# A gated linear attention with two mixture layers: fewer weight conversions in the attention front, a three-step schedule for the second chunk, and another order in the gate

## The chip, the cores and the metric

The kernel runs on one core of one Trainium2 chip. The metric is the time of one execution on the device in microseconds (us). Three runs of the kernel before gave 1474.3, 1478.15 and 1478.42, median 1478.15. A separate execution was profiled; it took 1473.71 us.

## The reference

Attention with a gated state, per batch and head, 768 steps, head size 48:

```
f = 1 / (1 + exp(-f_logit))
state = f[t] * state + outer(k[t], v[t]);   y[t] = q[t] @ state
```

The heads are laid side by side (384 columns, 3072 tokens). Then a first layer with a rational activation, and a second with four experts:

```
h = x @ w_in                                  # 384 -> 2048
g = (a0 + a1 h + a2 h^2 + a3 h^3) / (1 + |b0||h| + |b1| h^2 + 1e-6)
x = g @ w_out                                 # 2048 -> 384
p = probs / (sum(probs) + 1e-9)
out = sum over e of p[:, e] * (relu(x @ w1[e]) @ w2[e])   # 384 -> 1024 -> 384
```

All is float32. The weights of the first layer (w_in, w_out) arrive as pairs of 32-bit words and have to be turned into float32 on the chip.

## The kernel before, in words

The tokens are cut into six chunks of 128 time steps by four batches (512 columns each). Per chunk the kernel does attention in four blocks (one per batch), the first layer in 16 slots of 128 hidden columns, and the second layer in 4 x 8 slots. A matmul in full precision is made of three passes: an operand is split into a high part (ScalarE) and the rest (GpSimd for weights, VectorE for activations), and high x high, low x high, high x low are summed; so a slot's first or second product of 128x512 is nine matmuls. Weights that are used again are stored to DRAM in split form ("ws<-w") and read back.

One loop runs over steps v from -25 to 192, with tau = v + 19. It emits the instructions of all engines by hand, in this order; each engine runs its own in order, so a wait on one engine holds what is behind it. There are three parts.

- *Front*, tau -6 to -2: Att.first takes the four blocks of the first chunk, one per step, with the block before finishing in the same step. On VectorE: w, scans, the first halves of the step's conversions, the masking of the old block, newton1, newton2, q_hat, the second halves of the conversions, finish. k_hat (k times g) and the conversion's last product are on GpSimd. warm() issues matmuls with no use for their result. The block after the next is loaded at the end of a step by SP, behind the step's stores.
- *Fill*, tau -1 to 18: the first layer on the first chunk with plain float32 matmuls, one slot per step: fill_in(tau + 1), then fill_out(tau - 2), six matmul instructions each; the rational gate (gate_in on ScalarE, gate_step on VectorE and ScalarE) lies between: a tile is "new" in one step and "old" in the next. Slot j needs its converted weights at tau = j - 1. CONV1 gives the step of each slot's conversion. A conversion has a first half (L731, L732 on VectorE, L733, L734 on ScalarE) and a second half (L736, L737 on VectorE, the product at L739, a store to w1s, and for odd slots the load of the next raw pair).
- *Main*, v from -1: step v emits in2 (v + 1) and out2 (v - 1) of the second layer, and where first_mix_steps says, in1 and out1 of the first layer for the next chunk, whose gate runs in gate_step. The attention of chunks 1 to 5 is threaded in: Att.t0 gives a block's start step and Att.stage what it issues k steps later: k = 1 exp, w, scans; 2 inverse, k_hat (GpSimd), newton1, newton2; 3 q_hat (GpSimd); 4 scores and masking; 5 and later the transposes of k, the y products, the update of the state and the transposes of y. PA is threaded between the matmuls of the step's first in2, PB between those of out2; DVE1, ACT0, ACT1, POOL1 and REST are places in the step for the other engines. loads() issues f at k = -1, k and q at k = 0, v at k = 2.

Chunk 1 starts a block every two steps from v = -4 and uses two PSUM banks, 6 and 7: scores in both, then the transposes of k in 6 and y in 7, then the update in 6 and the transposes of y in 7. Bank 5 belongs to in1 (h1), and in the fill banks 5 to 7 hold the gate's q. Weights for the main part are loaded from tau = 10 on.

Of the kernel before, what the change touches and what calls it, by code (L numbers as in the profile page):

```python
# [8 lines left out]
F32 = mybir.dt.float32  # L9
F32R = mybir.dt.float32r  # L10
# [3 lines left out]
ALU = mybir.AluOpType  # L14
# [3 lines left out]
NB, NH, S, D = 4, 8, 768, 48  # L18
# [4 lines left out]
PR = 112  # L23
# [307 lines left out]

R = 14
AHEAD = 8
CONV1 = (-6, -5, -5, -4, -4, -3, -3, -2, -2, -1, 0, 1, 2, 3, 4, 5)
NRAW = 8
LAST = NCH * NE * NJ2
FILL = NJ1 + 3
# [1 line left out]
PA, PB, ACT0, ACT1, POOL1, DVE1, REST = range(7)  # L339


def first_mix_steps():


    when, groups = {}, {}
    for c in range(1, NCH):
        p = NE * NJ2 * (c - 1)
        if c == 1:
            at = [8, 9, 10, 12, 14, 15, 16, 17, 18, 19, 20, 21, 23, 24, 25, 26]
            ends = (16, 20, 24, 29)  # L350
        else:
            at = [2, 3, 4, 5] if c == 2 else [-1, 1, 3, 5]
            at += [7, 9, 11, 13, 15, 17, 19, 21, 23, 24, 25, 26]
            ends = (8, 16, 24, 29)
        for j, s in enumerate(at):
            when[p + s] = (c, j)
        for n, s in enumerate(ends):
            groups[p + s] = (c, n)
    return when, groups
# [37 lines left out]
class Block:  # L397


    def __init__(self, att, c, b):  # L400
        self.att, self.nc, self.c, self.b = att, att.tc.nc, c, b
        if c == 0:
            self.pa, self.pk, self.py = att.bank_sets[b % 2]
            self.px = self.pk
        else:
            self.pa, self.py = self.pk, self.px = att.pair
        self.last = c == NCH - 1
# [30 lines left out]

    def k_hat(self):
        k = self.k[0:PR]  # L440
        self.nc.gpsimd.tensor_tensor(out=k, in0=k, in1=self.g[0:PR], op=ALU.mult)

    def newton1(self):
        nc, gm, g = self.nc, self.att.gm[0:PR], self.g[0:PR]
# [92 lines left out]
class Att:  # L537
# [16 lines left out]
    @staticmethod  # L554
    def t0(c, b):
        if c == 1:
            return -4 + 2 * b
        if c == 2:
            return 5 + 7 * b
        return NE * NJ2 * (c - 1) - 9 - 8 * (3 - b)  # L560

    def start(self, fetch):
# [80 lines left out]
    def stage(self, blk, k):  # L643
        rs = range(NP)
        if k == 1:
            return {ACT0: [blk.exp], DVE1: [blk.w], REST: [blk.scans]}
        if k == 2:
            return {ACT0: [blk.inverse], POOL1: [blk.k_hat], DVE1: [blk.newton1], REST: [blk.newton2]}
        if k == 3:
            return {POOL1: [blk.q_hat]}  # L650
        if k == 4:
            return {PA: [blk.all_scores], REST: [blk.masked]}
        keys = [] if blk.last else [partial(blk.k_t, r) for r in rs]
        upd = [] if blk.last else [partial(blk.update, r) for r in rs]
        copy = [] if blk.last else [blk.k_copy]
        end = ([] if blk.last else [blk.finish]) + [blk.x_lo]
        xt = [partial(blk.x_t, m) for m in range(3)]
        if blk.c == 1:
            if k == 5:
                return {PA: keys + blk.y_parts(*rs), ACT1: copy + [blk.y_copy], PB: upd + xt, REST: [blk.x_hi] + end}  # L660
            return {}
        if k == 5:
            return {PB: keys + blk.y_parts(*rs), REST: copy}
        if k == 6:
            return {PA: upd, ACT1: [blk.y_copy]}
        if k == 7:
            return {PA: xt, ACT1: [blk.x_hi], REST: end}
        return {}
# [13 lines left out]
def fused(ctx, tc, aps, consts, gm, dp, prep, flag_op):  # L682


    nc = tc.nc
    w1, w2, out = aps["w1"], aps["w2"], aps["out"]
    sc, pn, ident, mask = consts
# [5 lines left out]
    def pool(name, bufs):  # L693
        return ctx.enter_context(tc.tile_pool(name=name, bufs=bufs))

    wp, x2p, sp, op, pbp, tp, osp = (pool(n, k) for n, k in (
        ("wp", R), ("x2p", 2), ("s1p", 1), ("op", 1), ("pbp", 1), ("tp", 2), ("osp", 2)))
    g1p, g2p, gp = pool("g1p", QC1), pool("g2p", 3), pool("gp", 2)
    att = Att(ctx, tc, aps, consts, gm, banks)
# [7 lines left out]
    raw, temp, w1f = {}, {}, {}  # L707
# [3 lines left out]
    def fetch():  # L711
        i = fetched[0]
        if i < NJ1:
            fetched[0] += 2
            pl, tag = (att.xp, "x") if i == 4 else (x2p, "x2")
            t = pl.tile([128, 2, 2 * SW], I32, tag=tag, name="raw")
            for a in range(2):
                raw[i + a] = t[:, a]
                nc.sync.dma_start(out=raw[i + a], in_=w1[i + a].bitcast(I32))

    def conv(i, stage):
        if stage == 0:
            t = spare_pools[i % 3].tile([128, 2 * SW], F32, tag=("o", "s1", "pb")[i % 3], name="t")
            temp[i] = t
        f = temp[i]
        p, m = f[:, 0:SW], f[:, SW:2 * SW]
        pi, mi = p.bitcast(I32), m.bitcast(I32)
        words = raw[i].rearrange("p (n w) -> p n w", w=2)
        lo, hi = words[:, :, 0], words[:, :, 1]
        if stage == 0:  # L730
            nc.vector.tensor_scalar(pi, hi, 0x7FF00000, None, ALU.bitwise_and)  # L731
            nc.vector.tensor_scalar(mi, hi, 0x000FFFFF, None, ALU.bitwise_and)  # L732
            nc.scalar.activation(out=pi, in_=pi, func=AF.Relu, scale=8.0, bias=sc[:, 7:8])  # L733
            nc.scalar.activation(out=m, in_=mi, func=AF.Identity, scale=2.0 ** -20, bias=sc[:, 8:9])  # L734
        else:
            nc.vector.scalar_tensor_tensor(out=pi, in0=hi, scalar=-2 ** 31, in1=pi, op0=ALU.bitwise_and, op1=ALU.bitwise_or)  # L736
            nc.vector.scalar_tensor_tensor(out=m, in0=lo.bitcast(U32), scalar=2.0 ** -52, in1=m, op0=ALU.mult, op1=ALU.add)  # L737
            w1f[i] = wp.tile([128, SW], F32, tag="w", name="wf")
            nc.gpsimd.tensor_tensor(out=w1f[i], in0=m, in1=p, op=ALU.mult)  # L739
            nc.sync.dma_start(out=w1s[i], in_=w1f[i])  # L740
            if i % 2:
                fetch()

    def conv_ops(tau):
        fs = [[], []]
        for i in range(NJ1):
            for k in range(2):
                if tau == CONV1[i] + k * (CONV1[i] > NB - 8):
                    fs[k].append(partial(conv, i, k))
        return fs  # L750

# [51 lines left out]
    x2, hps, act1, act2 = {}, {}, {}, {}  # L803
# [88 lines left out]
    def gate_step(new, old, ops):  # L892

        if old:
            q0, r0, y0, _ = gate.pop(old[:2])
            nc.vector.scalar_tensor_tensor(out=q0, in0=q0, scalar=QC, in1=r0, op0=ALU.add, op1=ALU.mult)  # L896
        if new:
            q, r, y, h = gate[new[:2]]
            nc.vector.scalar_tensor_tensor(out=q, in0=q, scalar=sc[:, 5:6], in1=r, op0=ALU.mult, op1=ALU.add)  # L899
            nc.scalar.activation(out=r, in_=q, func=AF.Ln, bias=sc[:, 6:7])  # L900
            nc.scalar.activation(out=r, in_=r, func=AF.Exp, scale=-1.0)
        if old:
            nc.vector.scalar_tensor_tensor(out=q0, in0=q0, scalar=2.0, in1=r0, op0=ALU.subtract, op1=ALU.mult)
        if new:
            nc.vector.tensor_tensor(out=y, in0=y, in1=h, op=ALU.mult)  # L905
        if old:
            if old[0] == 0:
                gh = g1p.tile([128, 512], F32, tag="gh", name="g")
                nc.vector.scalar_tensor_tensor(out=gh, in0=y0, scalar=sc[:, 3:4], in1=q0, op0=ALU.subtract, op1=ALU.mult)
                act1[old[:2]] = gh  # L910
            else:
                nc.vector.scalar_tensor_tensor(out=q0, in0=y0, scalar=sc[:, 3:4], in1=q0, op0=ALU.subtract, op1=ALU.mult)  # L912
        for f in ops[DVE1]:
            f()
        if new:
            nc.vector.scalar_tensor_tensor(out=y, in0=y, scalar=sc[:, 2:3], in1=h, op0=ALU.subtract, op1=ALU.mult)  # L916
        for f in ops[ACT1] + ops[POOL1]:
            f()
        if old and old[0]:
            gh = g1p.tile([128, 512], F32R, tag="gh", name="gh")  # L920
            gl = g1p.tile([128, 512], F32R, tag="gl", name="gl")
            nc.scalar.copy(out=gh, in_=q0)  # L922
            nc.vector.tensor_tensor(out=gl, in0=q0, in1=gh.bitcast(F32), op=ALU.subtract)  # L923
            act1[old[:2]] = (gh, gl)

# [90 lines left out]
    for v in range(-FILL - 6, LAST + 1):  # L1016
        tau = v + FILL
        ops = att.begin(v)
        if tau == -5:
            prep()  # L1020
        if tau + 6 <= NB:
            att.first(tau + 6, conv_ops(tau) if tau + 6 < NB else [[], []])
# [16 lines left out]
        new = ready[0] if ready else None  # L1039
        if new:  # L1040
            gate_queue.remove(new)
        old, pend_old = pend_old, new
# [5 lines left out]
        c, k = v // (NE * NJ2) - 1, v % (NE * NJ2)  # L1048
# [217 lines left out]
```

## Time and profile before

| | us |
|---|---|
| median of three runs (lowest, highest) | 1478.15 (1474.3, 1478.42) |
| profiled execution, and its span | 1473.71, 1471.9 |
| TensorE busy in the span | 1386.3 (94%) |
| VectorE, ScalarE, GpSimd busy | 907.8, 679.0, 306.3 |
| mean granted TensorE clock | 0.967 of full speed |

PE is TensorE's matmul part, PEld its weight loads, DVE VectorE, ACT ScalarE, POOL GpSimd, SP the engine that issues most DMAs; L731 is line 731 of the kernel before. Busy time of PE counts a matmul at whatever clock it was granted, so a stage with a clock below 1.00 holds less work than its busy time says. Times are from the start of the span.

### The profile page before, as it was taken

How to read it: one execution, taken by the hardware profiler on the slowest of the kernel's cores; microseconds unless marked ns; L12 is line 12 of the kernel's file. 1: busy time of each engine (PE TensorE's matmuls, PEld its weight loads, DVE VectorE, ACT ScalarE, POOL GpSimd, SP SyncE). 2: the span in 40 equal slices, each digit the busy share in tenths (PEclk: the TensorE clock that was granted, in tenths of full speed). 3: DMA queues.
4: the chain of work that ended last, by engine and by line, in shares of the span. 5: the costliest groups of instructions: out<-in, count | busy, mean ns of one | idle time of the engine just before them, and what ended most of it. 6: DMA issues, size and time to landing. Idle time of an engine off the chain costs nothing.

```text
span 1471.9 us, 18283 instructions
## 1 busy us (share of the span) xinstructions
PE 1386.3 (94%) x6502; PEld 1112.8 (76%) x6502; DVE 907.8 (62%) x1395; ACT 679.0 (46%) x1160; POOL 306.3 (21%) x265
## 2 busy tenths in 40 slices
PE   5859989999989999999999999999999999999997
PEld 5723477877768888878888878888878888888885
DVE  7799844678784666575666675666675645562222
ACT  3367623767562644552553552553552643451111
POOL 3232324465643002012001012001012001111010
PEclk8779969999999999999999999999999999999998
DMA  7352635767787566666666565665665766667660
GB/s 259 122 189 79 232 118 189 237 221 250 247 296 257 180 190 204 181 185 219 188 201 189 185 206 179 215 206 186 196 206 174 227 193 194 181 204 235 193 183 24
DMA packets 115699, 287.80 MB, mean 196 GB/s; under 512 B 13104, under 2 KB 31888, under 8 KB 114832
## 3 DMA queue, kind: packets, MB, share of 16 engines
q1 hardware_dynamic: 115024, 286.36, 60.4%
q8 instruction: 54, 0.88, 0.3%
q14 instruction: 45, 0.37, 0.1%
q10 hardware_dynamic: 576, 0.18, 0.0%
HBM read 237.69 MB, written 48.81 MB: 195 GB/s over the span
## 4 chain that ended last, share of the span: by engine, by line
PE 74%; DVE 14%; ACT 3%; DMA 3%; issue 3%; POOL 2%; SPq 1%; ACTq 0%; DVEq 0%; POOLq 0%
PE bank L839 34%; PE bank L829 31%; PE bank L484 2%; PE bank L489 1%; DMA ws<-w 1%; DVE t L737 1%; PE bank L867 1%; POOL w L786 1%; DVE g L431 1%; PE bank L874 1%; DVE t L732 1%; PE bank L460 1%; PE bank L500 1%; DVE q L899 1%; DVE y L905 1%
## 5 line engine op out<-in xcount | busy, mean ns | idle before, releaser
L829 PE MATMUL bank<-x,w 128*128 128x512 f32 x2448 | 616.6, 397 | 9.1 <-DVE gl L932 7.2
L829 PEld LDWEIGHTS bank<-x,w 128*128 128x128 f32 x2448 | 457.0, 190 | 104.4 <-DVE gl L932 9.5
L839 PE MATMUL bank<-gh,w 128*128 128x512 f32 x1632 | 529.6, 400 | 5.0 <-DVE t L968 5.0
L839 PEld LDWEIGHTS bank<-gh,w 128*128 128x128 f32 x1632 | 304.6, 189 | 66.8 <-DVE t L968 5.9
L839 PE MATMUL bank<-gl,w 128*128 128x512 f32 x816 | 324.5, 398 | 0.0
L932 DVE SCALAR_TENSOR_TENSOR gl<-bank,gh 128x512 fp32r<-128x512 f32 x192 | 131.6, 686 | 128.0 <-ACT gh L931 128.0
L969 POOL TENSOR_TENSOR o<-o,t 128x512 f32<-128x512 f32 x69 | 87.4, 1295 | 511.8 <-DVE t L968 511.8
L839 PEld LDWEIGHTS bank<-gl,w 128*128 128x128 f32 x816 | 154.1, 189 | 30.7
L899 DVE SCALAR_TENSOR_TENSOR q<-q,sc,r 128x512 f32<-128x512 f32 x80 | 63.7, 797 | 177.6 <-ACT r L888 177.5
L931 ACT ACTIVATE gh<-bank 128x512 fp32r<-128x512 f32 x192 | 113.7, 594 | 125.2 <-PE bank L829 125.2
L786 POOL TENSOR_TENSOR w<-rawbuf,w 128x384 fp32r<-128x384 f32 x96 | 105.3, 1121 | 102.5 <-ACT w L785 76.0
L922 ACT CAST gh<-q 128x512 fp32r<-128x512 f32 x80 | 49.6, 620 | 157.5 <-DVE q L912 156.8
L883 ACT COPY h<-bank 128x512 f32<-128x512 f32 x80 | 46.9, 586 | 133.1 <-PE bank L829 132.5
L484 PEld LDWEIGHTS bank<-v,am 128*128 128x128 f32 x384 | 70.7, 221 | 22.1 <-DVE am L471 17.5
L484 PE MATMUL bank<-v,am 128*128 128x48 f32 x384 | 65.2, 282 | 16.9 <-DVE am L471 16.9
L923 DVE TENSOR_TENSOR gl<-q,gh 128x512 fp32r<-128x512 f32 x80 | 55.4, 692 | 36.3 <-ACT gh L922 35.7
L968 DVE TENSOR_TENSOR t<-bank,pb 128x512 f32<-128x512 f32 x69 | 46.0, 687 | 42.4 <-PE bank L839 23.1
L986 DVE TENSOR_TENSOR s<-s,bank 128x512 f32<-128x512 f32 x45 | 30.6, 682 | 66.9 <-PE bank L839 66.9
L867 PE MATMUL bank<-x,wf 128*128 128x512 f32 x96 | 48.8, 649 | 20.0 <-DVE y L916 19.3
L534 POOL TENSOR_TENSOR s<-am,i 48x192 f32<-48x192 f32 x32 | 16.3, 510 | 240.2 <-DVE am L533 239.0
L896 DVE SCALAR_TENSOR_TENSOR q<-q,r 128x512 f32<-128x512 f32 x80 | 66.0, 825 | 0.0
L900 ACT ACTIVATE r<-q,sc 128x512 f32<-128x512 f32 x80 | 58.0, 725 | 17.1 <-DVE q L899 9.1
(100 smaller groups left out, 1495.6 us busy)
## 6 DMA issues: line engine op xcount, KB each, us to landing
w<-ws SPq DMA_DIRECT2D x448, 384.0 KB, 3.6
ws<-w SPq DMA_DIRECT2D x96, 384.0 KB, 3.8
raw<-in_w_dram SPq DMA_DIRECT2D x16, 768.0 KB, 6.9
rawbuf<-in_w_dram SPq DMA_DIRECT2D x64, 192.0 KB, 3.5
f<-in_qkf_dram SPq DMA_DIRECT2D x24, 256.0 KB, 3.7
k<-in_qkf_dram SPq DMA_DIRECT2D x24, 256.0 KB, 4.0
q<-in_qkf_dram SPq DMA_DIRECT2D x24, 256.0 KB, 4.2
w1s<-wf SPq DMA_DIRECT2D x16, 384.0 KB, 5.6
```

Of the source, the lines that this page charges most:

```text
L484: self.nc.tensor.matmul(self.py[:, o:o + D], self.am[a][:, r], self.v[:, o:o + D], start=(self.c == 0 and r == 0 and a == 0), stop=(r == N ...
L786: nc.gpsimd.tensor_tensor(out=t[:, 1], in0=r, in1=t[:, 0].bitcast(F32), op=ALU.subtract)
L829: nc.tensor.matmul(ps, a[:, o], b[:, kk, :], start=(n == 0), stop=(n == 8))
L839: nc.tensor.matmul(acc[m], a[:, o], b, start=(start and n == 0), stop=(stop and n == last))
L867: nc.tensor.matmul(ps, w[:, kk * 128:(kk + 1) * 128], att.x[0][:, kk, :], start=(kk == 0), stop=(kk == 2))
L896: nc.vector.scalar_tensor_tensor(out=q0, in0=q0, scalar=QC, in1=r0, op0=ALU.add, op1=ALU.mult)
L899: nc.vector.scalar_tensor_tensor(out=q, in0=q, scalar=sc[:, 5:6], in1=r, op0=ALU.mult, op1=ALU.add)
L900: nc.scalar.activation(out=r, in_=q, func=AF.Ln, bias=sc[:, 6:7])
L923: nc.vector.tensor_tensor(out=gl, in0=q0, in1=gh.bitcast(F32), op=ALU.subtract)
L931: nc.scalar.activation(out=gh, in_=h, func=AF.Relu)
L932: nc.vector.scalar_tensor_tensor(out=gl, in0=h, scalar=0.0, in1=gh.bitcast(F32), op0=ALU.max, op1=ALU.subtract)
L969: nc.gpsimd.tensor_tensor(out=o[c][:, m], in0=o[c][:, m], in1=t, op=ALU.add)
```

## The change

1. CONV1: the first four conversions go one to each of the front's steps (before: one, two, two, and two first halves), the other twelve are spread over tau -2 to 13. Those of the front do their last product on VectorE, and so does k_hat for chunk 0.
2. Chunk 1's blocks start every three steps from v = -6 and use banks 5, 6 and 7: scores in 5 and 7, the transposes of k in 6, y in 7, update in 5, transposes of y in 6. The transposes of k and the y products move from PA to PB of k = 5; update and the rest move to k = 6. The scores are threaded after the first matmul of the in2 group, not after the ninth. in1 of chunk 1 runs at steps 10, 11, 12, 13 where it was 8, 9, 10, 12; chunk 2's blocks start at 6, 12, 19, 26 where it was 5, 12, 19, 26.
3. gate_step issues the old tile's operations first, with its copy to gh right behind, then ACT1, then the new tile's, then DVE1 and POOL1, and gl last.

```
-CONV1 = (-6, -5, -5, -4, -4, -3, -3, -2, -2, -1, 0, 1, 2, 3, 4, 5)
+CONV1 = (-6, -5, -4, -3, -2, -1, 0, 1, 3, 4, 5, 7, 8, 9, 11, 12)
...
-            at = [8, 9, 10, 12, 14, 15, 16, 17, 18, 19, 20, 21, 23, 24, 25, 26]
+            at = [10, 11, 12, 13, 14, 15, 16, 17, 18, 19, 20, 21, 23, 24, 25, 26]
...
+        elif c == 1:
+            self.pa, self.pk, self.py = att.bank_sets[0]
+            self.px = self.pk
...
     def k_hat(self):
         k = self.k[0:PR]
-        self.nc.gpsimd.tensor_tensor(out=k, in0=k, in1=self.g[0:PR], op=ALU.mult)
+        eng = self.nc.gpsimd if self.c else self.nc.vector
+        eng.tensor_tensor(out=k, in0=k, in1=self.g[0:PR], op=ALU.mult)
...
         if c == 1:
-            return -4 + 2 * b
+            return -6 + 3 * b
         if c == 2:
-            return 5 + 7 * b
+            return (6, 12, 19, 26)[b]
...
         if k == 4:
-            return {PA: [blk.all_scores], REST: [blk.masked]}
+            return {PA: [blk.all_scores] + [lambda: None] * (8 * (blk.c == 1)), REST: [blk.masked]}
...
         if blk.c == 1:
             if k == 5:
-                return {PA: keys + blk.y_parts(*rs), ACT1: copy + [blk.y_copy], PB: upd + xt, REST: [blk.x_hi] + end}
+                return {PB: keys + blk.y_parts(*rs), REST: copy}
+            if k == 6:
+                return {PA: upd, ACT1: [blk.y_copy], PB: xt, REST: [blk.x_hi] + end}
             return {}
...
-            nc.gpsimd.tensor_tensor(out=w1f[i], in0=m, in1=p, op=ALU.mult)
+            eng = nc.vector if CONV1[i] < NB - 6 else nc.gpsimd
+            eng.tensor_tensor(out=w1f[i], in0=m, in1=p, op=ALU.mult)
...
-                if tau == CONV1[i] + k * (CONV1[i] > NB - 8):
+                if tau == CONV1[i] + k * (CONV1[i] >= NB - 6):
```

gate_step after the change (STT stands for nc.vector.scalar_tensor_tensor):

```
if old:
    STT q0 = (q0 + QC) * r0;  STT q0 = (2 q0 - ...) * r0
    if old[0]: STT q0 = (y0 - a0) * q0;  gh = nc.scalar.copy(q0)
    else:      STT gh = (y0 - a0) * q0;  act1[old[:2]] = gh
ops[ACT1]
if new:
    STT q = q * |b1| + r;  ScalarE Ln, Exp;  y = y * h;  STT y = (y - a1) * h
ops[DVE1], ops[POOL1]
if old and old[0]: gl = q0 - gh
```

## Rows read from the trace of the kernel before

**Rows 1.** Windows by stage: busy us (count) per engine, clock, DMA share, GB/s.
```profile
0.00:68.40 68.40, 44.66 (x288) 42.40 (x288) 49.78 (x91) 26.23 (x40) 18.50 (x17) 0.75 0.56 205
68.40:178.30 109.90, 89.36 (x195) 37.43 (x195) 100.68 (x146) 71.80 (x113) 32.84 (x19) 0.92 0.45 154
178.30:267.20 88.90, 80.45 (x425) 66.88 (x426) 45.16 (x72) 30.80 (x63) 37.50 (x39) 0.85 0.52 176
267.20:430.00 162.80, 151.82 (x735) 124.13 (x733) 122.06 (x171) 111.41 (x206) 91.06 (x83) 0.99 0.72 250
430.00:1400.00 970.00, 958.79 (x4591) 792.10 (x4592) 573.80 (x890) 428.85 (x723) 121.56 (x107) 1.00 0.64 199
```

**Rows 2.** Groups by shape on VectorE, 0 to 67 us: busy us, mean ns, idle before.
```profile
L732 DVE TENSOR_SCALAR t<-raw 128x768 int32<-128x768 int32 x7 | 7.1, 1013 | 0.0
...
L737 DVE SCALAR_TENSOR_TENSOR t<-raw,t 128x768 f32<-128x768 uint32 x5 | 6.4, 1275 | 0.0
...
L736 DVE SCALAR_TENSOR_TENSOR t<-raw,t 128x768 int32<-128x768 int32 x5 | 4.8, 955 | 2.8 <-ACT t L733 2.8
L731 DVE TENSOR_SCALAR t<-raw 128x768 int32<-128x768 int32 x7 | 3.8, 544 | 2.4 <-DMA raw<-in_w_dram 2.4
L424 DVE TENSOR_SCALAR f<-f 112x512 f32<-112x512 f32 x4 | 3.6, 911 | 0.7 <-ACT f L420 0.6
L456 DVE TENSOR_TENSOR q<-q,i 112x512 f32<-112x512 f32 x4 | 2.8, 692 | 0.1
...
L1189 DVE TENSOR_SCALAR psum__65<-psum__65 128x24 f32<-128x24 f32 x1 | 1.7, 1717 | 0.0
```

**Rows 3.** Timeline of the front: start, us, engine, line, operation, idle before.
```profile
5.13 1.37 DVE L431 TENSOR_TENSOR_SCAN g<-f,sc 112x128 f32<-112x128 f32 x4
...
31.65 2.80 DVE L431 TENSOR_TENSOR_SCAN g<-f,sc 112x128 f32<-112x128 f32 x4
...
33.62 0.44 SPq L411 DMA_DIRECT2D f<-in_qkf_dram  x1
...
40.57 0.63 ACT L420 ACTIVATE f<-f 112x512 f32<-112x512 f32 x1 [4.74 <-DMA f<-in_qkf_dram]
...
55.20 3.65 PE L484 MATMUL bank<-v,am 128*128 128x48 f32 x16 [3.18 <-DVE am L471]
...
68.41 2.84 PE L867 MATMUL bank<-x,wf 128*128 128x512 f32 x6 [0.57 <-ACT x L516]
```

**Rows 4.** Timeline of the fill.
```profile
86.81 5.49 PE L867 MATMUL bank<-x,wf 128*128 128x512 f32 x6 [12.87 <-DVE y L916]
...
110.30 0.69 DVE L896 SCALAR_TENSOR_TENSOR bank<-bank,r 128x512 f32<-128x512 f32 x1
...
116.73 0.70 DVE L896 SCALAR_TENSOR_TENSOR bank<-bank,r 128x512 f32<-128x512 f32 x1
...
166.24 10.46 PE L874 MATMUL bank<-g,wf 128*128 128x512 f32 x24
```

**Rows 5.** TensorE's waits, 180 to 260 us: total us, times, longest.
```profile
PE bank L476 <- DVE am L471: 7.6, 3, 3.1
```

**Rows 6.** Timeline of the third stage.
```profile
205.61 3.65 DVE L446 SCALAR_TENSOR_TENSOR i<-g,r 112x512 f32<-112x512 f32 x1 [0.56 <-POOL w L786]
...
247.15 0.40 PE L829 MATMUL bank<-x,w 128*128 128x512 f32 x1
...
255.64 2.23 PE L829 MATMUL bank<-x,w 128*128 128x512 f32 x9
...
259.75 4.24 PE L829 MATMUL bank<-x,w 128*128 128x512 f32 x18
...
263.92 1.16 PE L460 MATMUL bank<-q,k 48*128 48x128 f32 x16
```

**Rows 7.** Groups by shape on GpSimd, 0 to 67 us.
```profile
L739 POOL TENSOR_TENSOR wf<-t 128x768 f32<-128x768 f32 x5 | 11.4, 2279 | 22.8 <-DVE t L737 22.8
```

**Rows 8.** Groups by shape on VectorE, 67 to 130 us.
```profile
L732 DVE TENSOR_SCALAR t<-raw 128x768 int32<-128x768 int32 x9 | 9.8, 1091 | 0.0
```

More of the change, by code (lines that the diff above doesn't have):

```diff
@@ L896, in gate_step @@
             nc.vector.scalar_tensor_tensor(out=q0, in0=q0, scalar=QC, in1=r0, op0=ALU.add, op1=ALU.mult)
+            nc.vector.scalar_tensor_tensor(out=q0, in0=q0, scalar=2.0, in1=r0, op0=ALU.subtract, op1=ALU.mult)
+            if old[0]:
+                nc.vector.scalar_tensor_tensor(out=q0, in0=y0, scalar=sc[:, 3:4], in1=q0, op0=ALU.subtract, op1=ALU.mult)
+                gh = g1p.tile([128, 512], F32R, tag="gh", name="gh")
+                nc.scalar.copy(out=gh, in_=q0)
+            else:
+                gh = g1p.tile([128, 512], F32, tag="gh", name="g")
+                nc.vector.scalar_tensor_tensor(out=gh, in0=y0, scalar=sc[:, 3:4], in1=q0, op0=ALU.subtract, op1=ALU.mult)
+                act1[old[:2]] = gh
+        for f in ops[ACT1]:
+            f()
         if new:
@@ L901, in gate_step @@
             nc.scalar.activation(out=r, in_=r, func=AF.Exp, scale=-1.0)
-        if old:
-            nc.vector.scalar_tensor_tensor(out=q0, in0=q0, scalar=2.0, in1=r0, op0=ALU.subtract, op1=ALU.mult)
-        if new:
             nc.vector.tensor_tensor(out=y, in0=y, in1=h, op=ALU.mult)
[L906 to L915, printed above, removed]
             nc.vector.scalar_tensor_tensor(out=y, in0=y, scalar=sc[:, 2:3], in1=h, op0=ALU.subtract, op1=ALU.mult)
-        for f in ops[ACT1] + ops[POOL1]:
+        for f in ops[DVE1] + ops[POOL1]:
             f()
         if old and old[0]:
-            gh = g1p.tile([128, 512], F32R, tag="gh", name="gh")
             gl = g1p.tile([128, 512], F32R, tag="gl", name="gl")
-            nc.scalar.copy(out=gh, in_=q0)
             nc.vector.tensor_tensor(out=gl, in0=q0, in1=gh.bitcast(F32), op=ALU.subtract)
```

## The prediction

> **What bounds the kernel now.** I read the table by stages first [rows 1]. From 430 us on TensorE is busy 958.8 of 970 us at a granted clock of 1.00: nothing that the change could free is to be had there, and what is won earlier is kept, because that part is a fixed queue of matmuls. The loss lies ahead of it: in the front (0 to 68.4 us, clock 0.75), in the fill (68.4 to 178.3) and in the steps in which the second chunk's attention runs (178.3 to 267.2, clock 0.85). So I asked of each of these three what ends last.
>
> In the front it is VectorE. The groups by shape [rows 2] are to be read for two means of one operation. L736 and L737 are the same instruction on the same shape, yet 955 ns against 1275; L732 needs 1013 ns and its twin L731 544. The excess comes from the few instances that stand behind a GpSimd instruction: (1013 - 544) x 7 = 3.3 us, (1275 - 955) x 5 = 1.6, L1189 1.7 where 24 elements need 0.2, so 1.5; L424 at 911, though it has fewer elements than the 544 ns of L731, at least 1.5; and four scans that took 2.80 where the first four took 1.37, 1.4 [rows 3]. Together 9.3 us. At the end of the front TensorE takes over: from 55.20, when the third block's masked scores are there, to 68.41, the first fill matmul [rows 3].
>
> In the fill VectorE first works off a backlog of conversions before the first gate, and TensorE waits 12.9 us for that gate's end, until 86.81; then a step lasts 116.73 - 110.30 = 6.43 us while the conversions last, and 10.46 / 4 = 2.6 us per group of six matmuls, two groups a step, at the end [rows 4].
>
> In the third stage TensorE's waits name one place: L476, the transposes of k, waits 7.6 us in three stalls for L471, the masking [rows 5]. Ahead of L471 on VectorE stands L446, which took 3.65 us [rows 6] where an operation of its shape, L456, takes 0.69; it started while GpSimd multiplied k and split weights. After each stall the clock falls: 0.85 over 88.9 us means about 27 us at the lower level (half speed), 13 us of work lost.
>
> **The change part by part.** Sums are made against the profiled execution, 1473.7 us (span 1471.9 and 1.8 around it); the median of the runs is 4.4 higher, the lowest 0.6.
>
> *Front.* Before, the first attention step has one conversion, the second and third two each, the fourth two first halves. After, one whole conversion in each of the four. Taken away on the path: one conversion in step two and one in step three, at 2.7 us each on VectorE (955 + 955 + 544 + 544 ns less about 0.08 that neighbouring records overlap), one first half (1.0) in step four before the masking; 6.4. Taken away with GpSimd: the 9.3 us of blocked instructions. Added on VectorE: three multiplications of k (the first lies in its wait for raw weights), priced like L456, 692 ns [rows 2]: 2.1; three multiplications of a converted slot on the path, 128x768, priced like L736: 2.9 (GpSimd took 2.28 for one [rows 7]). The second half of the fourth conversion, 2.9 with its product, lies under TensorE's work after 55.20 and costs nothing while that takes over 5 us. Net 6.4 + 9.3 - 2.1 - 2.9 = 10.7. Two things can take some back. The third step's conversion waits for ScalarE, which waits for the fourth block's f: issued at 33.62, used at 40.57 [rows 3], 6.9 us. After, SP issues it at about 28 (behind one store instead of two, and the raw pair) and it lands near 34.5; VectorE is there at 34.5 too, and ScalarE still has its exponential and the conversion's first activation to do, so a wait of about 1.4 us stays, as today. Lower and upper bounds of that load, 5 and 8.5 us, make it -1.5 to +1.5. Second, TensorE's clock in the last front step. I take 11: fill starts at 57.4.
>
> *Fill.* It now holds twelve conversions instead of nine and two halves, spread to step 13. Lead-in: the fifth conversion, then the first gate at about 61.5, 4 us after the fill's start (a late half and a first half, 2.7, and a wait for ScalarE). From there VectorE is the bound: a step with the gate alone is 6.43 - 2.7 = 3.75, less than TensorE's 5.2; with a conversion 6.43. Steps 0 to 13 hold 13 1/2 gates (50.6), eleven second halves at 1.75 (19.3) and ten first halves at 0.95 (9.5): 79.4, so 140.9. The last product is still GpSimd's, 2.1 us (2.28 in the mean with the blocked ones [rows 7]); then fill_in(15), 2.6, and, queued behind it on TensorE, four fill_out at 2.6: 156.0. The first block's scores now stand ahead of the last of them: 1.1 more. GpSimd's product can still block L732 when a first half follows a second half in one step, which is so eight times; in today's fill the mean of L732 is 1091 for nine [rows 8], an excess of 4.9, three blocked of nine at 1.6. I take 4.8 for the eight; bounds 0 and 12.8. Fill ends at 161.9, against 176.7 (166.24 + 10.46) [rows 4]: 14.8 earlier, 11 of them from the front and 3.8 here.
>
> The Trainium skill, SBUF — State Buffer, section "SBUF: two separate sides", says that VectorE and GpSimd hold a shared port pair as an exclusive lock for a whole instruction, so that the later one fully blocks. By that rule all eight would be blocked and the fill would end 8 us later than I sum; the trace has only three of nine. What it would do here is in the first rival.
>
> *Second chunk's attention.* Today two steps per block and two banks: scores and transposes of k share bank 6, so L476 must wait for the masking, and the next block's L446 stands in front of that masking in the same step. After, three steps per block and banks 5, 6, 7: the transposes go to a bank that the masking doesn't read, half a step later, and L446 falls into a step whose masking is done. L446 may still be blocked 3 us; late next would be the gl of the following step, which TensorE needs only a full step on. The loads of q and k no longer queue on SP for banks' readers of the block before. Price of the stage if TensorE never waits: eighteen matmuls take 4.17 (259.75 to 263.92), so nine take 2.1; the step from 247.15 to 255.64, 8.49, less 4.17, and scores of 1.1 make 5.4 for a block [rows 6]. Up to 267.2 there are eleven first and nine second products of nine matmuls: 20 x 2.08 = 41.7; four blocks 21.6, less the scores already done, 1.1: 62.2. Today the same work takes 88.9 less one in1 group and one set of scores of the third chunk, 3.2: 85.7. I allow 4 for new waits (four blocks, one of the old stall's 2.5 in every second one): 66.2, a gain of 19.5. Bounds: 23.5 if none, 0 if every block stalls as now.
>
> *Gate order.* The old tile's three operations now fill the time in which VectorE waits for ScalarE's squares, and gl no longer waits for gh. It issues nothing more. Up to 430 us TensorE is busy 151.8 of 162.8 [rows 1], so at most 11 could come, and as much as 4 be lost, since y_copy and x_hi now stand on ScalarE ahead of Ln and Exp. The nearest row is the stage after, where TensorE has no slack: I take 0. The later start of in1 (steps 10 to 13 in a row) costs nothing in matmuls; a step then has three groups of nine on TensorE, 6.2 us, under which ScalarE's longer row of activations has to lie, and if it doesn't, the 4 us above are the price.
>
> Sum: 11 + 3.8 + 19.5 = 34.3: 1439.4 against the profiled execution, 1443.9 against the median, 1440 against the lowest run. I say 1442.
>
> **The rivals.** (1) The lock takes it back in the fill: eight blocked first halves, 12.8 in place of 4.8, so 8.0 more, and L446 of the first block, now among the last gates, blocked as in [rows 6], 3.0: 1453. For it: the front's excess in [rows 2]. Against: [rows 8]. It is also what the rule of the Trainium skill's page SBUF — State Buffer, named above, would make of this fill. (2) The wait moves: scores are now issued after the first matmul of a group and not after the ninth, so a late q_hat on GpSimd holds eight matmuls behind it, and the clock falls as now. Half of the third stage's gain, 10, is lost: 1452. For it: GpSimd is busy 37.5 us in that stage and splits stand ahead of q_hat. Against: q_hat has a step more than L446's 3.65 needs. (3) Slower: TensorE stays at half speed through the fill. A group then takes 5.49 (86.81) [rows 4], a step 11 in place of 6, so 5 lost a step; from the seventh of the fourteen steps on the change loses, with eleven of them it ends at 1495. For it: the lead-in leaves TensorE idle about 4 us again before its fourth group. Against: today it recovers after 12.9 us idle, and a mean clock of 0.92 leaves at most 18 us of the stage at half speed.
>
> **How the numbers follow.** Forecast 0.62, with its own range 1433 to 1449; rival 1 0.14, rival 2 0.15, rival 3 0.06, and 0.03 for rival 1 with the third stage's whole gain lost and the f load at its upper bound, 1442 + 11 + 19.5 + 1.5 = 1474, no change. A measurement can tell about 0.3%, 4.4 us, from no change. Faster 0.91, same 0.03, slower 0.06. Range 1428 to 1462: below it lies the case that the gate order frees waits too, above it rival 3, the case of no change, and rivals 1 and 2 together (1463).
>
> **What would show it.** First L867 at 56 to 60 us and no GpSimd instruction between 2 us and the fifth conversion; L732 and L737 in the front at 0.55 and 0.95; the last fill_out near 160; L476 waiting for L471 no more and a clock near 1.00 in the 90 us after. Wrong would be: a TensorE wait of over 2 us on L460 for q_hat, L867 waiting for a product at fill_in(13) to (15) by more than 5 us in sum, or a stage after 267 longer than before.

## The result, and the profile after

The changed kernel takes 1455.8 us in the median of four runs (1448.4 to 1457.1), the kernel before 1478.0; the ratio is 0.9845, 95% interval 0.9808 to 0.9881, 22 us. I had said 1442: faster as forecast and inside the whole range, but outside the forecast's own (1433 to 1449), nearest to rival 1's 1453, and 14 us of the gain are missing. Lines of the changed kernel: the first half of a conversion is L737 and L738 (L731, L732 before), the second L742 and L743, its product L746; the fill's matmuls L874 and L881; the gate's old tile L903, L904, L911, the new one L917, L920, L921; scores L464, transposes of k L480, masking L475; h copied by L890.

The windows by stage, which answer to [rows 1] (busy us and count of TensorE, its weight loads, VectorE, ScalarE, GpSimd, then the clock, DMA share, GB/s):

```profile
0.00:56.00 56.00, 37.66 (x289) 35.31 (x289) 42.18 (x91) 21.08 (x34) 1.69 (x8) 0.85 0.65 239
56.00:177.40 121.40, 93.67 (x210) 39.23 (x211) 117.60 (x161) 76.64 (x117) 32.09 (x20) 0.93 0.43 141
177.40:240.00 62.60, 62.28 (x385) 52.61 (x385) 34.36 (x59) 26.41 (x54) 35.37 (x36) 1.00 0.73 250
240.00:410.00 170.00, 158.50 (x746) 129.19 (x745) 125.42 (x168) 112.37 (x210) 91.50 (x83) 0.95 0.67 233
410.00:1380.00 970.00, 959.31 (x4596) 792.04 (x4595) 581.53 (x896) 429.00 (x729) 121.10 (x106) 1.00 0.64 200
```

The front is 12.4 us shorter. The stage of the second chunk's attention now runs at a clock of 1.00, with TensorE busy 62.3 of 62.6 us. But the fill between them lasts 121 us in place of 108, and VectorE is busy for 117.6 of them: that is where the rest went.

TensorE's row at the stages' borders (start, us, operation, count, idle before it in brackets and what ended it):

```profile
55.96 2.84 PE L874 MATMUL bank<-x,wf 128*128 128x512 f32 x6 [0.57 <-ACT x L520]
...
152.87 2.84 PE L874 MATMUL bank<-x,wf 128*128 128x512 f32 x6 [3.33 <-POOL wf L746]
161.26 4.54 PE L874 MATMUL bank<-x,wf 128*128 128x512 f32 x6 [2.97 <-POOL wf L746]
...
174.54 2.84 PE L881 MATMUL bank<-g,wf 128*128 128x512 f32 x6
176.82 2.47 PE L836 MATMUL bank<-x,w 128*128 128x512 f32 x8
...
239.96 2.23 PE L836 MATMUL bank<-x,w 128*128 128x512 f32 x9
```

The fill begins at 55.96 (68.41 before [rows 3]) and ends at 177.4 (176.7 before [rows 4]). The tenth step ends at 239.96; the same point lay at about 264.0 before (267.2 in [rows 1] less 3.2 for a group of nine matmuls and a set of scores that had gone ahead there).

Two steps of the fill on VectorE, which answer to the 110.30 and 116.73 of [rows 4]:

```profile
66.16 2.17 DVE L738 TENSOR_SCALAR t<-raw 128x768 int32<-128x768 int32 x1
68.24 0.69 DVE L903 SCALAR_TENSOR_TENSOR bank<-bank,r 128x512 f32<-128x512 f32 x1
68.96 0.70 DVE L904 SCALAR_TENSOR_TENSOR bank<-bank,r 128x512 f32<-128x512 f32 x1
69.70 0.75 DVE L911 SCALAR_TENSOR_TENSOR g<-y,sc,bank 128x512 f32<-128x512 f32 x1
70.36 0.75 DVE L917 SCALAR_TENSOR_TENSOR bank<-bank,sc,r 128x512 f32<-128x512 f32 x1
71.02 0.68 DVE L920 TENSOR_TENSOR y<-y,bank 128x512 f32<-128x512 f32 x1
71.74 0.75 DVE L921 SCALAR_TENSOR_TENSOR y<-y,sc,bank 128x512 f32<-128x512 f32 x1
72.40 0.95 DVE L742 SCALAR_TENSOR_TENSOR t<-raw,t 128x768 int32<-128x768 int32 x1
73.27 0.95 DVE L743 SCALAR_TENSOR_TENSOR t<-raw,t 128x768 f32<-128x768 uint32 x1
74.14 0.55 DVE L737 TENSOR_SCALAR t<-raw 128x768 int32<-128x768 int32 x1
74.61 2.17 DVE L738 TENSOR_SCALAR t<-raw 128x768 int32<-128x768 int32 x1
76.70 0.68 DVE L903 SCALAR_TENSOR_TENSOR bank<-bank,r 128x512 f32<-128x512 f32 x1
```

A step takes 8.46 us (68.24 to 76.70) where it took 6.43. No line has idle time in front of it; instead L738 takes 2.17 where its twin takes 0.55, and the six gate operations, 68.24 to 72.40, take 4.16. The same six of the kernel before, whose order was old, new, old, new, old, new:

```profile
103.86 0.69 DVE L896 SCALAR_TENSOR_TENSOR bank<-bank,r 128x512 f32<-128x512 f32 x1
104.45 0.75 DVE L899 SCALAR_TENSOR_TENSOR bank<-bank,sc,r 128x512 f32<-128x512 f32 x1
105.11 0.69 DVE L903 SCALAR_TENSOR_TENSOR bank<-bank,r 128x512 f32<-128x512 f32 x1
105.71 0.68 DVE L905 TENSOR_TENSOR y<-y,bank 128x512 f32<-128x512 f32 x1
106.31 0.74 DVE L909 SCALAR_TENSOR_TENSOR g<-y,sc,bank 128x512 f32<-128x512 f32 x1
106.96 0.74 DVE L916 SCALAR_TENSOR_TENSOR y<-y,sc,bank 128x512 f32<-128x512 f32 x1
107.62 0.95 DVE L736 SCALAR_TENSOR_TENSOR t<-raw,t 128x768 int32<-128x768 int32 x1
```

Here they take 3.76. Read the starts, not the durations: those are the same, but an operation that uses the result of its neighbour starts later, L904 0.72 behind L903 where L899 starts 0.59 behind L896. (Later in the fill the changed order's six take 4.25.)

### The profile page after: what moved, and what is told of

The parts are those of the page before. It is cut to its first block, busy times and chain, and to the rows that moved or that the text cites. A ratio compares the mean times of both kernels' runs of the same rounds, so it can differ in the third digit from the quotient of the medians.

```text
span 1455.2 us, 18263 instructions
## 1 busy us (share of the span) xinstructions
PE 1375.7 (95%) x6502; PEld 1100.6 (76%) x6502; DVE 919.0 (63%) x1403; ACT 675.7 (46%) x1160; POOL 289.1 (20%) x257
## 4 chain that ended last, share of the span: by engine, by line
PE 74%; DVE 15%; POOL 3%; issue 3%; DMA 2%; ACT 2%; SPq 0%; POOLq 0%; ACTq 0%; DVEq 0%
PE bank L846 34%; PE bank L836 32%; PE bank L488 2%; DVE t L738 1%; PE bank L464 1%; PE bank L493 1%; POOL w L793 1%; DVE y L920 1%; POOL o L972 1%; DVE t L742 1%; DMA f<-in_qkf_dram 1%; DVE t L743 1%; DVE y L921 1%; PE bank L504 1%; DVE q L904 1%
## 5 line engine op out<-in xcount | busy, mean ns | idle before, releaser
L836 PE MATMUL bank<-x,w 128*128 128x512 f32 x2448 | 609.1, 395 | 9.2 <-DVE gl L935 7.3
L917 DVE SCALAR_TENSOR_TENSOR q<-q,sc,r 128x512 f32<-128x512 f32 x80 | 60.2, 752 | 156.6 <-ACT r L895 156.6
L890 ACT COPY h<-bank 128x512 f32<-128x512 f32 x80 | 46.9, 586 | 142.6 <-PE bank L836 142.1
L874 PE MATMUL bank<-x,wf 128*128 128x512 f32 x96 | 51.7, 682 | 28.3 <-DVE y L921 21.4
L488 PEld LDWEIGHTS bank<-v,am 128*128 128x128 f32 x384 | 64.9, 201 | 14.4 <-DVE am L475 9.9
L488 PE MATMUL bank<-v,am 128*128 128x48 f32 x384 | 60.3, 262 | 9.4 <-DVE am L475 9.4
L904 DVE SCALAR_TENSOR_TENSOR q<-q,r 128x512 f32<-128x512 f32 x80 | 65.5, 819 | 2.8
L906 DVE SCALAR_TENSOR_TENSOR q<-y,sc,q 128x512 f32<-128x512 f32 x80 | 64.8, 810 | 2.8
L903 DVE SCALAR_TENSOR_TENSOR q<-q,r 128x512 f32<-128x512 f32 x80 | 64.4, 805 | 0.0
```

The source lines that it names most:

```text
L488: self.nc.tensor.matmul(self.py[:, o:o + D], self.am[a][:, r], self.v[:, o:o + D], start=(self.c == 0 and r == 0 and a == 0), stop=(r == N ...
L836: nc.tensor.matmul(ps, a[:, o], b[:, kk, :], start=(n == 0), stop=(n == 8))
```

## The experiments

Theory A, formed on these rows: VectorE's row bounds the whole fill, and the change put two things on it, eight first halves blocked behind GpSimd's product (1.62 us each) and a gate step some 0.45 us longer. Rival B: the conversions are placed too late, whatever VectorE's row costs. Three groups of runs, on three chips; each was timed beside the kernel before on its own chip, so the ratios are what compares. "Fill ends" and "rest" (from there to the last instruction) are of the profiled execution.

```
kernel                 median   ratio (95%)              fill ends   rest
before                 1478.0   1                        176.7     1295.2
changed                1455.8   0.9845 (0.9808-0.9881)   177.4     1277.8
e1_half_first          1440.0   0.9729 (0.9698-0.9760)   165.4     1273.9
e2_old_gate            1442.2   0.9752 (0.9716-0.9788)   166.6     1273.6
e3_both                1435.5   0.9698 (0.9666-0.9730)   160.0     1274.0
e4_attention_only      1456.6   0.9849 (0.9814-0.9883)   179.8     1275.0
e5_gate_only           1484.2   1.0060 (1.0032-1.0088)   188.2     1293.5
e6_apart               1444.3   0.9795 (0.9750-0.9839)   169.8     1272.4
e7_early               1433.1   0.9712 (0.9670-0.9753)   157.1     1274.2
e8_old_gate_all        1441.8   0.9763 (0.9725-0.9801)   158.9     1280.8
e9_two_banks           1463.2   0.9914 (0.9882-0.9946)   178.3     1277.4
e10_three_banks        1480.5   1.0029 (1.0006-1.0053)   177.6     1302.2
e11_early_alone        1456.1   0.9875 (0.9838-0.9911)   180.6     1273.8
```

**First half ahead.**

```
-            for f in sum(reversed(conv_ops(tau)), []):
+            for f in sum(conv_ops(tau), []):
```

> The changed kernel with one edit: in a step of the fill the first half of the next conversion stands on VectorE ahead of the second half of this one, so that no first half stands right behind GpSimd's product. Theory A (VectorE bounds the fill; eight first halves of 2.17 us in place of 0.55 behind the product, 8 x 1.62 = 13.0 us, and a gate chain 0.45 us longer a step): all first halves at 0.55, the fill ends near 164.5 in place of 177.4, time 1456 - 13 = 1443 (1440 to 1447). Rival B (the conversions are simply placed too late, TensorE waits for them whatever VectorE's row costs): the waits for the product at the last two fill matmul groups stay, time within 3 us of 1456. Rival C (raw words or stores on the way slow these instructions, not GpSimd): still 2.17 in the new place, 1456.

Every first half falls to 0.55 but one, which takes 1.17 beside GpSimd's split of weights; the fill ends 12.0 us earlier, and 1440 is the lower end of what theory A gave. Rival C is out. What rival B named is what is left, one long wait for a late product:

```profile
142.40 5.38 PE L874 MATMUL bank<-x,wf 128*128 128x512 f32 x6 [4.95 <-POOL wf L746]
```

**The gate's old order back.** `gate_step` as it was before, parts one and two as changed.

> The changed kernel with the third part undone everywhere: the gate interleaves old and new tile as before. Theory A: a step's gate on VectorE takes 3.77 in place of 4.22 us, 13.5 steps, the fill ends 6 us earlier; after the fill nothing: 1450 (1447 to 1452). Rival D (the new order earns as much or more in the stages after the fill than it costs in it): 1455 or more, and TensorE's waits for the gates between 240 and 430 us longer than with the new order, by over 4 us in sum. Rival B: the fill's end does not move by more than 2 us.

It gains about twice what theory A gave: the fill ends 10.8 us earlier and lasts 14.6 us less (106.8 after 121.4), since in this profiled execution it starts 3.9 later, at 59.8; that comes from the front's clock and is taken up below. The six operations are back at 3.8, and, which nobody expected, only two of the eight first halves behind a product stay blocked, the first two; the other six take 0.55 to 0.59. GpSimd's rows show what happened to the lock, by which one of GpSimd's product and VectorE's first half stands still while the other runs (e2, two products with a first half behind them and one without):

```profile
69.73 2.05 POOL L746 TENSOR_TENSOR wf<-t 128x768 f32<-128x768 f32 x1 [4.39 <-DVE t L743]
77.79 2.54 POOL L746 TENSOR_TENSOR wf<-t 128x768 f32<-128x768 f32 x1 [6.00 <-DVE t L743]
84.24 1.81 POOL L746 TENSOR_TENSOR wf<-t 128x768 f32<-128x768 f32 x1 [3.91 <-DVE t L743]
```

Alone (84.24, no first half behind it) the product takes 1.81. At 69.73 the first half was blocked, at 77.79 it was not, and then the product took 2.54: GpSimd waited. One of the two waits in every such pair; which one changed with the gate's order. Six freed first halves at 1.62 and the shorter gate, 6, make 15.7 of which 14.6 are seen.

**Both.** The two edits together, the old order for tiles of the fill alone.

> The changed kernel with the first halves ahead of the second halves, as in the run before, and the gate's old order in the fill's steps alone; behind the fill the changed order stays. Theory A: the two terms add, 13 + 6: the fill ends near 158, 1437 (1433 to 1441). Rival E (with VectorE 19 us lighter TensorE or the last product becomes the bound): no more than 13 in all, 1443 or more.

The fill ends 17.4 us earlier, 1435.5: as theory A had it. The gains don't add (the fill lasts 12.2 us less in e1, 14.6 in e2, 17.8 here), because the old order already frees most of the first halves. TensorE again waits 3.85 for the product at 136.66, and its group then takes 5.49.

**The second part alone**, put on the kernel before.

> The kernel before with the second part alone: second chunk's attention in three steps per block on three banks, and the later start of its products. Theory A: this part carries all of the net gain, 22.7 us as measured between the fill's end and the tenth step: 1478 - 23 = 1455 (1452 to 1459). Rival F (it needs the front's lead or the gate's order as well): half, 1466 or more.

0.9849 beside 0.9845: this part alone gives all that the whole change gives. In the stage (179 to 243 us) no wait on the masking remains, and the clock is 1.00.

**The third part alone**, put on the kernel before.

> The kernel before with the third part alone: the gate finishes the old tile first. Theory A (in the fill this order costs VectorE 0.45 us a step and lets GpSimd's product go ahead of the first half every time): six steps with a conversion cost 6 x 0.45 and five more blocked first halves 5 x 1.6, 10.7 us later at the end of the fill, ratio to the kernel before 1.007 (1.004 to 1.010). Rival D (the order earns in the stages behind): 1.000 or less. Rival G (the later fill steps, bound by TensorE, take it up): 1.000 to 1.003.

Slower, 1.006: the fill ends 11.5 us later and lasts 11.0 longer (10.7 expected), and eight of eight first halves are blocked, three of eight before. The two steps show both costs in a kernel in which these places were free:

```profile
97.77 2.17 DVE L732 TENSOR_SCALAR t<-raw 128x768 int32<-128x768 int32 x1
99.86 0.69 DVE L896 SCALAR_TENSOR_TENSOR bank<-bank,r 128x512 f32<-128x512 f32 x1
...
104.02 0.95 DVE L736 SCALAR_TENSOR_TENSOR t<-raw,t 128x768 int32<-128x768 int32 x1
...
106.23 2.17 DVE L732 TENSOR_SCALAR t<-raw 128x768 int32<-128x768 int32 x1
```

**Dependent neighbours apart.** In the fill, g is moved between the new tile's product and the operation that uses it:

```
+            y = y * h
+            g = (y0 - s) * q0          # from ahead of the new tile
             y = (y - s) * h
```

> The changed kernel with one move in the fill's gate: the old tile's last operation stands between the new tile's product y times h and the operation that uses it, so that no two neighbours of the second half of the gate depend on each other; the first two of the old tile still stand together. Theory P (a dependent pair right ahead of the conversion decides that GpSimd's product goes ahead of the first half): blocked first halves fall from eight to two or three, the gate step from 4.22 to about 3.9, the fill ends near 167, time 1443 (ratio 0.975). Rival Q (what decides is which tile is finished first, not the neighbours): the first halves stay at 2.17, only the gate is shorter, 4 us, 1452 (ratio 0.981).

The gate step is 3.90 as said (76.26 to 80.16), but the lock comes out as neither had it: six of eight first halves still blocked. The fill ends 7.6 us earlier, which the gate (0.32 in 13 1/2 steps, 4.3) and two freed first halves (3.2) account for; the ratio, 0.9795, lies between the two theories'. Here are two of the same surroundings:

```profile
92.38 0.55 DVE L737 TENSOR_SCALAR t<-raw 128x768 int32<-128x768 int32 x1
92.85 2.17 DVE L738 TENSOR_SCALAR t<-raw 128x768 int32<-128x768 int32 x1
...
100.58 0.55 DVE L737 TENSOR_SCALAR t<-raw 128x768 int32<-128x768 int32 x1
101.05 0.55 DVE L738 TENSOR_SCALAR t<-raw 128x768 int32<-128x768 int32 x1
```

The products start 0.17 and 0.16 us behind L737 in the two cases, so the order of arrival doesn't tell them apart either. What decides it is open.

**Earlier conversions on the best version.**

```
-CONV1 = (-6, -5, -4, -3, -2, -1, 0, 1, 3, 4, 5, 7, 8, 9, 11, 12)
+CONV1 = (-6, -5, -4, -3, -2, -1, 0, 1, 2, 3, 4, 6, 7, 8, 9, 10)
```

> The version with first halves ahead and the gate's old order in the fill, and its conversions placed earlier: CONV1 goes on from 1 with 2, 3, 4, 6, 7, 8, 9, 10 in place of 3, 4, 5, 7, 8, 9, 11, 12. Theory B' (once VectorE's row is short, the last products are late by their place in the schedule): TensorE's wait of 3.85 us for the last product and the half-speed group behind it, 2.65, go, the fill ends near 154, 1430 (ratio 0.966). Theory A alone (VectorE's row is the bound however it is spread): the fill ends within 2 us of 160, 1434 to 1437 (ratio 0.970).

The waits for late products are gone and the fill ends at 157.1, 2.9 us earlier: about half of what B' gave. By ratio (0.9712 and 0.9698) it isn't told apart from the version above; both are the fastest here, some 20 us under the changed kernel.

**The gate's old order behind the fill too.**

> First halves ahead, and the gate's old order everywhere, behind the fill too. If the gate's order is worth nothing behind the fill: ratio within 0.003 of the version that keeps the changed order there (0.970), the time from the fill's end to the last instruction 1274 within 3 us. Rival D (the changed order frees waits behind the fill): slower by 4 us or more than that version.

Slower than e3 by 0.0065, over 4 us, as rival D says, though the two were timed on different chips and their intervals just overlap; and most of the loss sits in one place, 1050 to 1075 us:

```profile
1050.00:1075.00 25.00, 23.07 (x106) 0.81 0.42 127
```

(columns: TensorE busy, clock, DMA share, GB/s); the same 25 us of e3 show 24.05 busy at 1.00. And e2, which has the old order everywhere too, has a rest of 1273.6 beside 1273.9 of e1 with the new one. So the order behind the fill may be worth 0 or 7 us; that stays open.

**Two banks, and three banks, alone.** The second part less its third bank; and the third bank without the rest:

```
+        elif c == 1:
+            self.pa, self.pk, self.py = att.bank_sets[0]
+            self.px = self.pk
```

> The kernel before with the second part alone, less its third bank: three steps per block of the second chunk's attention, but scores and transposes of k share one bank of two, as before. Theory S (the schedule carries the gain: the transposes of k come half a step after the masking, whatever bank they write): no stall on the masking, 62 to 64 us from the fill's end to the end of the tenth step, ratio 0.985 (0.982 to 0.988). Rival K (the banks carry it): stalls of 2 us and more on the masking come back in two blocks or more, the clock falls, half the gain is lost: ratio 0.992 or more.

> The kernel before with the third bank alone: two steps per block of the second chunk's attention as before, the transposes of k in a bank that the masking does not read. Theory S: four transposes later TensorE needs the masked scores themselves, so the stall moves from the transposes to the products with the masked scores and keeps its length less 0.5 us a block: ratio 0.998 to 1.000. Rival K: the stall goes, the stage falls by 10 us or more: ratio 0.993 or less.

With three banks alone the stall only moves, as theory S had it, from the transposes to the products with the masked scores:

```profile
PE bank L492 <- DVE am L474: 6.8, 3, 2.8
```

7.6 before [rows 5]. The time, 1.0029, is above the 0.998 to 1.000 that theory S gave: the clock of the stretch is 0.81 (177.6 to 268 us), beside 0.85 before (176.7 to 267), and why it is lower is open. With two banks and the new schedule the profiled execution shows no such wait and a clock of 1.00 through the stage: the schedule removes the stall, not the bank. From the fill's end to the end of the tenth step it takes 64.7 us (243.05 - 178.3), 2 more than with the third bank in e4. Its time is less clear: 0.9914 lies between the two theories' ranges, the eight runs spread from 1457.5 to 1467.2, and the profiled one (1457.6) is among the fastest. The two fastest were granted a mean clock of 0.975, the others 0.966 to 0.973; where they lose it no trace shows. So what the third bank adds to the schedule (0.9849 with it in e4, on another chip) stays open.

**Earlier conversions on the changed kernel**, the same line and nothing else.

> The changed kernel with its conversions placed earlier and nothing else: CONV1 goes on from 1 with 2, 3, 4, 6, 7, 8, 9, 10 in place of 3, 4, 5, 7, 8, 9, 11, 12. Theory A (VectorE's row bounds the fill): first halves follow a second half in ten steps in place of eight, 2 x 1.62 = 3.2 us more on VectorE, the waits for the last products go but TensorE waits as long for gates: fill ends between 175 and 181, time 1454 to 1459 (ratio 0.984 to 0.987). Rival B (the places of the last conversions bound it): TensorE's two waits of 3.3 and 3.0 us for the last products go, the fill ends near 171, 1450 or less (ratio 0.981 or less).

The fill ends at 180.6; TensorE no longer waits for a product, but for gates instead, and ten first halves are blocked. Rival B alone is out for the changed kernel: 0.9875, its interval holds 0.9845.

## Why the prediction was right in sign and 14 us short

**Front: the size right, one of its two parts not in the sum.** First fill matmul at 55.96, 57.4 forecast. No instruction there is blocked, as these two rows show, beside the 1275 and 1013 of [rows 2]:

```profile
L743 DVE SCALAR_TENSOR_TENSOR t<-raw,t 128x768 f32<-128x768 uint32 x4 | 3.8, 950 | 0.0
...
L738 DVE TENSOR_SCALAR t<-raw 128x768 int32<-128x768 int32 x4 | 2.2, 554 | 0.0
```

VectorE's part is 9.7 us, where I had 10.7 to 11: the third block's products with the masked scores start at 45.51, at 55.20 before [rows 3]. The other 2.8 of the 12.4 are TensorE's clock, which I had listed only as something that might take back. The same work from there to the first fill matmul, as windows of the kernel before, the changed kernel and e2 (columns as in [rows 1]):

```profile
55.20:68.40 13.20, 12.64 (x92) 12.16 (x92) 4.79 (x11) 2.83 (x6) 0.00 (x0) 0.76 0.01 2
45.50:55.96 10.46, 9.88 (x92) 9.26 (x93) 7.33 (x14) 3.38 (x7) 0.00 (x0) 1.00 0.48 165
46.06:59.79 13.73, 13.20 (x92) 12.61 (x92) 7.37 (x13) 2.96 (x6) 0.00 (x0) 0.73 0.40 144
```

The front of e2 is the changed kernel's, instruction for instruction, and yet its clock there was 0.73 and its fill began at 59.8; so these 2.8 us are no sure part of the gain.

**Second chunk's attention: right, a little low.** From the fill's end to the end of the tenth step 62.6 us where I gave 66.2 and 62.2 without any wait; the 4 us of allowance weren't needed. No wait on the masking is left, as I had said. Rival 1 comes true in its term for the fill alone: L450 (L446 before) took 1.70 once, 0.7 else, under a TensorE that did not wait. Rivals 2 and 3 did not come: no wait on L464 for q_hat in that stage, and TensorE recovers between the fill's groups (mean clock 0.93).

**Fill: wrong, 15.5 us** (161.9 forecast, 177.4 measured). Three terms of its sum failed:
- "I take 4.8 for the eight". It is eight times 1.62, 13.0: rival 1's term, 8.2 more. The misreading is of [rows 8]: three of nine blocked (of eight, in fact: one of the nine, at 76.41, has no product beside it) looked like a rule that holds now and then. The product's own rows, which I didn't ask, say otherwise:

```profile
88.58 2.06 POOL L739 TENSOR_TENSOR wf<-t 128x768 f32<-128x768 f32 x1 [4.40 <-DVE t L737]
96.63 2.54 POOL L739 TENSOR_TENSOR wf<-t 128x768 f32<-128x768 f32 x1 [6.00 <-DVE t L737]
...
129.00 1.81 POOL L739 TENSOR_TENSOR wf<-t 128x768 f32<-128x768 f32 x1 [4.05 <-DVE t L737]
```

The first two are of the kernel before, with a blocked first half (2.06) and a free one (2.54), the third stands alone. The lock was there every time; in the free cases GpSimd paid. The Trainium skill, SBUF — State Buffer, section "Who interferes with whom", says just that, that one of the two fully blocks and that the order of issue decides which; these rows bear out the first half of it, and e6 shows two outcomes at the same order of start.
- "A step with the gate alone is 6.43 - 2.7 = 3.75". That is the price in the old order. In the new one it is 4.16 to 4.25: about 0.45 for 13 1/2 gates, 6 us. I had priced the gate's new order by "it issues nothing more", and looked for its effect only behind the fill.
- The end: from the last second half on VectorE (159.21) to the fill's end it takes 18.2 us where I had queued 16.2, because the last fill_in, behind a wait of 2.97 for its product, took 4.54 where such a group takes 2.84 (rows at 161.26 and 55.96). With the wait of 3.33 at 152.87 TensorE waited 6.3 us for products, over the 5 that I had named as a sign of being wrong.

The three make 16 of the 16.9 us by which the fill outlasts my sum (121.4 us, 104.5 forecast); it began 1.4 earlier than forecast.

**Gate order: wrong, and by the runs the size of the whole error.** I took 0 with -11 to +4. Parts one and two without it take 1442.2 (e2), which is the 1442 that I forecast for all three; with it 1455.8. That the two agree so closely is partly luck, as e2's fill began 2.4 us later than I had said and the stage behind it was 3.6 shorter; but its fill lasted 106.8 us beside the 104.5 of my sum, so with the old order the sum holds to some 2 us. Alone the new order costs 0.6% (e5). Both failed terms of the fill are its doing: the dependent neighbours, and most of the lost locks. How an order of independent operations comes to decide the lock is not settled.

**Behind the tenth step** the profiled execution of the changed kernel loses about 7 us to that of before (1455.2 - 240.0 = 1215.2 against 1471.9 - 264.0 = 1207.9): a stage after 267 longer than before was another sign of being wrong that I had named. Some 4 of the 7 are longer waits in the stage's first steps. TensorE's two longest in e4, 280 to 305 us (total, times, longest):

```profile
PE bank L844 <- DVE t L973: 3.6, 1, 3.6
PE bank L834 <- ACT h L888: 2.1, 1, 2.1
```

With 0.9 for gl and 0.7 for q_hat they make 7.3. In the same steps the changed kernel waits 3.7, 1.9 and 1.6 for gl, 7.2; the kernel before 2.7 and 0.8, 3.5 (290 to 332 us). e4 has the old gate order, so this comes with part two and not with the gate; that the first products' later start does it is likely, but no run has that alone. I had put the price at 4 if ScalarE's row didn't fit. With the rest goes the clock: 0.83 from 360 to 380 us, where the kernel before has 1.00 at the same distance behind its tenth step (384 to 404). By medians little is left of the 7 us, if the tenth step ends alike in every run (1455.8 - 240.0 and 1478.0 - 264.0 differ by 2), as the profiled execution of before was below all four of its timed runs and that of after the slowest of four.

## What to carry to other kernels

Where an engine's row has no gaps, reordering is not free: price the new order's start-to-start distances, and put no operation next to the one whose result it uses. A blocked instruction shows on one of two engines, so ask both before you call a lock occasional. And time the parts of a change one by one: here the second part gave 22 us (e4), the first about 14 (e2 less e4, as no run has it alone), and the third took 14 back.

## What the runs showed of the hardware that I had not expected

- VectorE operations of 128x512 that use their neighbour's result start 0.12 to 0.21 us later than the same ones with another operation between them (0.72 and 0.74 to 0.81 against 0.59 to 0.60 behind the 0.69 us operations); three such places make 0.4 to 0.5 us a gate. In e6 two of the three pairs are parted, and the gate takes 3.90.
- Between GpSimd's 128x768 product (1.81 us alone) and VectorE's 128x768 first half (0.55), the product starting 0.16 to 0.24 us behind the conversion's first operation, either may go first: 2.06 and 2.17, or 2.54 and 0.55. Blocked were eight of eight in the changed kernel and in e5, ten of ten in e11, six of eight in e6, three of eight in the kernel before, two of eight in e2.
- Gate operations with one operand in PSUM behind the same product were not slowed in the fills that I read (L903 0.67 to 0.73 in seven of them); putting them there is what e1 does.
